# First projections in another order of x's tiles, and two sets of loads moved back

## The chip, the core and the metric

The kernel runs on one core of a Trainium2 chip. The metric is the device time of one execution in microseconds (us), given as the median of several runs. A core has five engines that each take their own instructions in order: TensorE (PE, matrix products; its weight loads are listed as PEld), VectorE (DVE), ScalarE (ACT), GpSimd (POOL) and SyncE (SP). SP here does nothing but issue DMA transfers, one after the other. The engines meet only through semaphores.

## The reference

The input x has 2048 tokens of 640 channels. Two branches are computed from it and mixed by a gate:

```python
g = _sigmoid((x * gate_w).sum(-1, keepdims=True))
a = _A_ref(x, A_wq, A_wk, A_wv, A_wo, A_beta)   # attention in 4 segments of 512 tokens, with a memory
b = _B_ref(x, B_w_r, B_w_i)                     # 2-D real FFT, times W = w_r + i*w_i, inverse FFT
return g * a + (1 - g) * b
```

Branch A has 32 heads of 20 channels. Within a segment it is causal softmax attention; beside it a linear memory of the segments before is read with phi(q) = q + 1 or exp(q), and updated with phi(k) and v. `sigmoid(beta)` weighs the two parts for each head, and a last product with `wo` closes the branch. Branch B transforms tokens and channels, multiplies by 2048 x 321 complex weights (the spectral weights), and transforms back.

## The kernel before

**How the work is cut.** Segment by segment (`s` = 0 to 3), `project` (L966) makes q, k and v from the transposed tokens `xT`, which the DMA delivers in five channel tiles `c` = 0 to 4 of 128 channels; `attend` (L1221) takes heads in groups of four: `qk_unit` (L1283) makes logits on PE, ACT takes their exponential into `ex` (L1319), POOL cuts out the causal mask (L1340), and PE multiplies by v. Branch B is spread between: `fold` (L946) adds and subtracts halves of the rows of x (`xsb`, through `xf`) on DVE and POOL, the products named `F1` (first transform, `fcat` against `xsb`) follow, then `D` and `T` (channel transform with table `big`, token transform with table `tt`), the multiplication with the spectral weights in `Wt` (L1496), and back through `Tb` and `Db`. `Db` (L1534) reads the columns of `big` from 1288 on, the inverse tables; `D` (L1480) reads the columns below.

**The first stage.** PE first runs ten products on zeros (`warm_up`, L847). Then `proj_direct` (L1017) makes q and k of the first two head groups (q0, k0, q1, k1) for segment 0, straight into the padded tile `qkp`: 4 x 5 operations named `projd`, one for each result and channel tile, the five of a result summing into one PSUM bank. Each result is copied out by one operation `ev_projd`. The weights `wq` and `wk` come in two parts: the first 192 columns (`ld_wqa`, `ld_wka`), which are all that `proj_direct` needs, and the other 448 (`ld_wqb`, `ld_wkb`), which every later projection (`proj_tile`, L1083) needs too. The x tiles come by three transposing DMAs: tiles 1 and 2 first, then tile 0, then 3 and 4, with `ld_wka` between the first two.

**beta.** `consts` (L929) takes exp(-beta) on ACT (L933) and from it, on DVE, 1 + exp(-beta) (L935), its reciprocal (L937) and their product (L938), which every copy of v (L1171) multiplies with.

**What sets the order.** All operations are recorded first and numbered in the order of recording. The table `ORDER` (from L633) is a list of numbers written out by hand: number v stands for operation v // 2, and v % 2 picks one of its engines where it may run on two (`copy_alts`: 0 is ACT, 1 is DVE). `Sched.schedule` (L117) walks it, keeps for each engine the order that the table gives, and picks PSUM banks, DMA semaphores and extra waits from its own table of costs; `emit` (L290) writes the instructions with their semaphore waits. So an engine never takes a later operation while an earlier one waits. The costs in `QUEUE` are the planner's alone; what it writes into the program for DMA is that a transfer waits for those issued some 1.6 MB ahead of it, and for the last user of its semaphore.

The programs of the engines are themselves fetched by DMA while they run, in 34 pieces of 16 KB (the queue called "instruction" in the profile); the longest by far is that of PE, with 4391 products and as many weight loads.

Of the kernel before, what the change touches and what calls it, by code (L numbers as in the profile page):

```python
# [12 lines left out]
P = 128  # L13
# [6 lines left out]
KD = 321  # L20
# [457 lines left out]
def dap(ap, off, *dims):  # L478
    return bass.AP(tensor=ap.tensor, offset=ap.offset + off, ap=[list(q) for q in dims])
# [25 lines left out]
class Kern:  # L505
# [84 lines left out]
    def dma(self, dst, src, nbytes, r, w, prio, tr=False, name="", after=(), queue="sp"):  # L590
# [24 lines left out]
        ("ld_big", 824320): (500.0, 2350.0, 16, 1350.0), ("ld_tt", 262144): (400.0, 1300.0, 16, 250.0), ("ld_tt", 524288): (400.0, 1750.0, 16, 600.0),  # L615
# [401 lines left out]
    def proj_direct(self, which, g, prio, xT, xb):  # L1017

        self.Sc.group += 1
        b = self.b  # L1020
        w, p0_ = (self.wq, 0) if which == "q" else (self.wk, 4 * L)
# [642 lines left out]
```

## Time and profile before

| what | value |
| --- | --- |
| median of 3 runs | 240.53 us |
| lowest and highest run | 238.36 and 241.71 us |
| profiled execution | span 238.5 us from first to last instruction; no other time is listed for it |
| PE busy | 94% of the span |
| ACT, DVE, POOL busy | 83%, 82%, 68% |
| mean granted clock of PE | 0.993 of full speed |
| moved by DMA | 42.18 MB in 59121 packets |

The span and the runs stand close: the profiled execution lies near the lowest of the three runs. A row of the timeline gives start, length, engine, line, the tile written and the tiles read, the shape and the number of instructions joined in the row; in brackets stands how long the engine was idle just before and what ended that. The lines L561, L571 and L573 are those of helpers (product, copy on ACT, copy on DVE), so such rows are told apart by their tiles. Successive rows of PE overlap, since products are pipelined; the distance from start to start is what one of them costs in a stream.

### The profile page before, as it was taken

Reading aid. Unit: us, or ns where it says so; the run is one execution under the profiler, and the core shown is the slowest. Engines: PE = TensorE matmul, PEld = TensorE weight load, DVE = VectorE, ACT = ScalarE, POOL = GpSimd, SP = SyncE. Lnnn points to the kernel's source line nnn. Section 1 sums busy time; section 2 is a strip of 40 time slices with the busy share of each in tenths; the row PEclk is TensorE's granted clock in tenths of the full one; section 3 lists DMA queues with packets and bytes.
Section 4 is the critical chain, followed back from the end, with each engine's and each line's share of the span. In section 5 each row is a group of like instructions: output and inputs, shape, how many; then the busy total and the mean of one; then the engine's idle time right before and its main releaser. Section 6 shows DMA issues by size and latency. Waiting matters only on the chain.

```text
span 238.5 us, 10359 instructions
## 1 busy us (share of the span) xinstructions
PE 224.9 (94%) x4391; PEld 142.1 (60%) x4391; DVE 194.8 (82%) x486; ACT 197.1 (83%) x233; POOL 162.0 (68%) x300
## 2 busy tenths in 40 slices
PE   6899999979999999999989999899999999989994
PEld 2576566656546666555657665456554456657794
DVE  0189998859999998899998888999999996847453
ACT  2079888969999998999989999988999888788820
POOL 8133139436769976737888979777998677786840
PEclk9799999999999999999999999999999999999999
DMA  7999659997879586493886683544998767492224
GB/s 148 294 330 271 196 148 171 231 230 157 230 181 231 156 214 184 122 269 100 179 230 186 182 278 87 174 124 138 200 273 210 187 142 109 95 82 85 74 70 110
DMA packets 59121, 42.18 MB, mean 177 GB/s; under 512 B 30212, under 2 KB 55364, under 8 KB 59076
## 3 DMA queue, kind: packets, MB, share of 16 engines
q1 hardware_dynamic: 58036, 40.96, 71.8%
q8 instruction: 34, 0.56, 1.0%
q10 hardware_dynamic: 1040, 0.57, 0.9%
q14 instruction: 11, 0.09, 0.1%
HBM read 23.32 MB, written 12.30 MB: 149 GB/s over the span
## 4 chain that ended last, share of the span: by engine, by line
PE 62%; ACT 13%; DMA 11%; DVE 9%; issue 2%; POOL 1%; SPq 1%; DVEq 0%; POOLq 0%
PE psum L561 54%; ACT ex L1319 11%; PE psum L559 8%; DMA qkp<-qk_scr 3%; DVE Pt L1496 2%; DMA u_scr<-ub 2%; DMA pkn<-phk 2%; DMA xT<-in_A_x_dram 2%; DMA tt<-tab_tt 2%; POOL ex L1340 1%; DMA dnc<-u_scr 1%; DVE qu L573 1%; SPq L594 1%; DVE Bt L573 1%; DVE phk L1141 1%
## 5 line engine op out<-in xcount | busy, mean ns | idle before, releaser
L1319 ACT ACTIVATE ex<-psum 128x2048 bf16<-128x2048 f32 (+4 forms) x92 | 138.5, 1506 | 13.2 <-PE psum L561 10.9
L1340 POOL TENSOR_SCALAR_AFFINE_SELECT ex<-ex 128x256 bf16<-128x256 bf16 (+2 forms) x224 | 118.6, 551 | 29.5 <-ACT ex L1319 6.1
L561 PE MATMUL psum<-qkp 20*64 20x64 bf16 (+5 forms) x1280 | 32.3, 270 | 3.5 <-ACT ex L1319 2.8
L561 PE MATMUL psum<-xT,wq 128*128 128x512 bf16 (+1 forms) x135 | 31.7, 423 | 2.3 <-DMA xT<-in_A_x_dram 2.0
L561 PE MATMUL psum<-xT,wk 128*128 128x256 bf16 (+1 forms) x280 | 32.6, 282 | 1.3 <-issue 1.3
L561 PEld LDWEIGHTS psum<-qkp 20*64 20x64 bf16 x1280 | 13.3, 103 | 21.9 <-ACT ex L1319 16.3
L1496 DVE TENSOR_TENSOR Pt<-psum,Wt 128x642 bf16<-128x642 f32 x32 | 25.4, 818 | 1.1 <-PE psum L561 0.9
L561 PE MATMUL psum<-wv,xT 128*32 128x321 bf16 (+3 forms) x390 | 26.1, 301 | 0.0
L561 PEld LDWEIGHTS psum<-xT,wk 128*128 128x128 bf16 (+1 forms) x280 | 20.5, 101 | 7.8 <-issue 4.0
L961 POOL TENSOR_TENSOR xsb<-xf 128x320 bf16<-128x320 bf16 (+2 forms) x11 | 8.1, 744 | 20.5 <-DVE xf L956 11.3
L559 PE MATMUL psum<-wo,oU 128*32 128x320 bf16 x480 | 21.5, 300 | 0.0
L573 DVE CAST ot<-psum 128x320 bf16<-128x320 f32 x22 | 10.4, 488 | 10.3 <-PE psum L559 7.2
L1171 DVE TENSOR_TENSOR va<-psum,ebx 128x320 bf16<-128x320 f32 x32 | 15.2, 487 | 4.2 <-PE psum L561 2.7
L561 PE MATMUL psum<-big,Cp 128*128 128x321 bf16 (+1 forms) x96 | 18.0, 302 | 0.2
L561 PEld LDWEIGHTS psum<-wv,xT 128*32 128x32 bf16 (+1 forms) x390 | 14.1, 96 | 6.3 <-issue 0.9
L561 PE MATMUL psum<-ex,va 128*32 128x64 bf16 (+3 forms) x576 | 17.6, 257 | 0.2
L561 PE MATMUL psum<-big,Ac 128*128 128x161 bf16 (+2 forms) x96 | 17.8, 256 | 0.0
L573 DVE CAST Bt<-psum 128x322 bf16<-128x322 f32 x28 | 14.3, 520 | 2.5 <-PE psum L561 2.3
L561 PEld LDWEIGHTS psum<-ex,va 128*32 128x32 bf16 x576 | 10.9, 96 | 8.7 <-POOL ex L1340 1.8
L561 PE MATMUL psum<-tt,Yt 128*128 128x256 bf16 (+1 forms) x96 | 15.8, 275 | 0.3 <-DVE Yt L1501 0.3
L1542 DVE TENSOR_TENSOR G<-eo,psum 128x320 bf16<-128x320 f32 x32 | 14.9, 477 | 1.2 <-ACT eo L571 0.5
L561 PEld LDWEIGHTS psum<-xT,wq 128*128 128x128 bf16 (+1 forms) x135 | 9.8, 105 | 10.2 <-DMA xT<-in_A_x_dram 2.5
(98 smaller groups left out, 392.0 us busy)
## 6 DMA issues: line engine op xcount, KB each, us to landing
qkp<-qk_scr SPq DMA_DIRECT2D x28, 160.0 KB
tt<-tab_tt SPq DMA_DIRECT2D x8, 512.0 KB, 4.5
qk_scr<-qu SPq DMA_DIRECT2D x12, 256.0 KB, 2.8
u_scr<-ub SPq DMA_DIRECT2D x12, 256.0 KB, 3.1
xsb<-in_A_x_dram SPq DMA_DIRECT2D x8, 320.0 KB, 5.0
oU<-u_scr SPq DMA_DIRECT2D x15, 128.0 KB, 3.6
out_dram<-ot SPq DMA_DIRECT2D x12, 160.0 KB
Wt<-in_B_w_r_dram SPq DMA_DIRECT2D x16, 80.2 KB, 4.7
```

Of the source, the lines that this page charges most:

```text
L559: h = e.matmul(dst, wt, r_, start=st, stop=sp_, **{**kw, "tile_position": (0, q), "skip_group_check": True})
L561: h = e.matmul(o_, l_, r_, start=st, stop=sp_, **kw)
L573: alts["dve"] = (lambda e: e.tensor_copy(dst(), src()), 67 + 1.04 * n, 68.0)
L594: return e.dma_start_transpose(d_, s_)
L961: self.either(lambda e, dst=dst, src=src, d0=d0, n=n, op=op: e.tensor_tensor(xs.ap(o + dst, [D, 2], [1, n]), xf.ap(src + d0, [321, 2], [1, ...
L1141: fmin = lambda e: e.tensor_tensor(dst(), dst(), et.ap(0, [1, L]), ALU.min)
L1171: self.one("dve", lambda e: e.tensor_tensor(va.ap(i * H * VW + h0 * VW, [VW, nh], [1, DH]), self.ps(bank, 0, [DH, nh], [1, DH]), self.ebx. ...
L1319: self.one("act", lambda e, d=d, q=q: e.activation(self.ex.ap(*d), self.ps(bank, *q), ACT.Exp, scale=SC), n, [bank], [self.exb(s, 2 * pr + ...
L1340: self.one("pool", lambda e: e.affine_select(self.ex.ap(e0 + d0, [1280, 4], [1, n], np_=np_), self.ex.ap(e0 + s0, [1280, 4], [1, n], np_=np_),
L1496: self.one("dve", lambda e, ri=ri, Pt=Pt, Wt=Wt, wo_=wo_, bank=bank: e.tensor_tensor(Pt.ap(ri * 322, [644, 2], [1, KD]), self.ps(bank, 0, ...
L1542: self.one("dve", lambda e, q=q, n2=n2, bank=bank, eo=eo: e.tensor_tensor(self.G.ap(n2 * D + 639 * q, [1 - 2 * q, 320]), eo.ap(q, [1, 320] ...
```

## The change

In `proj_direct` the five channel tiles are summed in the order 1, 2, 0, 3, 4; the start and stop flags of the sum follow the position and not the tile:

```diff
-        for c in range(5):
+        for step, c in enumerate((1, 2, 0, 3, 4)):
...
-                                c == 0 and o == 0, c == 4, {"tile_position": (0, 32 * hh), "skip_group_check": True})
+                                step == 0 and o == 0, step == 4, {"tile_position": (0, 32 * hh), "skip_group_check": True})
...
-            self.mms(items, [b("w" + which + "a"), xb[c], bank], [], prio + (0.0 if c < 3 else 0.45), name="projd", mode=2)
+            self.mms(items, [b("w" + which + "a"), xb[c], bank], [], prio + (0.0 if step < 3 else 0.45), name="projd", mode=2)
```

The load of `big` becomes two, and `Db` now waits for the second:

```diff
-        self.dma(lambda: self.big.ap(0, [1, 3220]), lambda: dap(self.tab["big"].ap(), 0, [3220, P], [1, 3220]),
-                 P * 6440, [], [self.b("big")], 5.0, name="ld_big")
+        self.dma(lambda: self.big.ap(0, [1, 1288]), lambda: dap(self.tab["big"].ap(), 0, [3220, P], [1, 1288]),
+                 P * 2576, [], [self.b("big")], 5.0, name="ld_big")
...
+        self.dma(lambda: self.big.ap(1288, [1, 1932]), lambda: dap(self.tab["big"].ap(), 1288, [3220, P], [1, 1932]),
+                 P * 3864, [], [self.b("inv")], 50.0, name="ld_inv")
...
-                    self.mms([(th, KD)], cpb + [b("big"), bank], [], prio, name="Db", mode=0)
+                    self.mms([(th, KD)], cpb + [b("inv"), bank], [], prio, name="Db", mode=0)
```

`ORDER` is written anew. The new load shifts the numbers of all later operations, so nearly every line of the table differs; operation by operation, the order of each engine changes only in this:

- **PE**: before, the twenty `projd` stand as q0 t0, k1 t0, q1 t0, k0 t0, q1 t1, q0 t1, k0 t1, q1 t2, q0 t2, q0 t3, k1 t1, k0 t2, k0 t3, k0 t4, q0 t4, k1 t2, k1 t3, k1 t4, q1 t3, q1 t4 (t is the channel tile). After: tiles 1 and 2 of q0, q1, k0, k1 in turn, then tile 0 of q0, k0, q1, k1, then tiles 3 and 4 of q0, k0, q1, k1. All that follows is the same.
- **ACT**: the copy of q1 moves here from DVE, between the copy of k0 and the first exponential. The exp(-beta) at L933, which stood right behind the first exponential, now stands behind the second; the copy of a k tile and an exp for phi (L1128) lie between.
- **DVE**: the copy of q0 stands ahead of the first two operations of `fold` instead of behind them; the copy of q1 is gone; all else is the same.
- **POOL**: no change.
- **SP**: three of the spectral loads `ld_W` for the second pair of row groups move back: two from right behind `ld_big` to behind the second tile pair of the third segment's xT, and one from behind `ld_hm` to behind the first store of `ub` (L1255). The new `ld_inv` stands some twenty transfers further, between the last pad load of the second segment's first half and the next `ld_W`.

More of the change, by code (lines that the diff above doesn't have):

```diff
@@ L614 @@
         ("ld_W", 41088): (600.0, 250.0, 16, 450.0), ("ld_W", 82176): (600.0, 500.0, 16, 550.0), ("ld_big", 659456): (500.0, 1750.0, 16, 950.0),
-        ("ld_big", 824320): (500.0, 2350.0, 16, 1350.0), ("ld_tt", 262144): (400.0, 1300.0, 16, 250.0), ("ld_tt", 524288): (400.0, 1750.0, 16, 600.0),
+        ("ld_big", 329728): (500.0, 950.0, 16, 1000.0), "ld_inv": (500.0, 1400.0, 16, 1000.0), ("ld_tt", 262144): (400.0, 1300.0, 16, 250.0), ("ld_tt", 524288): (400.0, 1750.0, 16, 600.0),
         ("ld_u", 131072): (595.0, 650.0, 16, 450.0), ("ld_u", 655360): (595.0, 1700.0, 16, 1800.0), ("ld_u", 262144): (595.0, 1000.0, 16, 900.0),
@@ L1027, in proj_direct, with th @@
                 for o, n, src in self.token_order(which, xT, c):
-                    def th(c=c, hh=hh, o=o, n=n, src=src):
+                    def th(c=c, hh=hh, o=o, n=n, src=src, step=step):
                         return (self.ps(bank, o, [1, n], p0=32 * hh, np_=32), w.ap(c * D + (4 * g + hh) * DH, [1, 32]), src(),
-                                c == 0 and o == 0, c == 4, {"tile_position": (0, 32 * hh), "skip_group_check": True})
+                                step == 0 and o == 0, step == 4, {"tile_position": (0, 32 * hh), "skip_group_check": True})
                     items.append((th, n / 4))
             items.sort(key=lambda q: q[0].__defaults__[2])
-            self.mms(items, [b("w" + which + "a"), xb[c], bank], [], prio + (0.0 if c < 3 else 0.45), name="projd", mode=2)
+            self.mms(items, [b("w" + which + "a"), xb[c], bank], [], prio + (0.0 if step < 3 else 0.45), name="projd", mode=2)
         self.Sc.op(self.copy_alts(lambda: pad.ap(p0_ + g * L, [1, L]), lambda: self.ps(bank, 0, [1, L]), L),
```

196 rows, old and new, of the table ORDER are left out of this document.

## The prediction

> **What bounds the kernel now.** I read the page first, then the chain that ended last in order of time, then the timeline engine by engine over the two stretches that the change touches.
>
> ```profile
> span 238.5 us, 10359 instructions
> PE 224.9 (94%) x4391; PEld 142.1 (60%) x4391; DVE 194.8 (82%) x486; ACT 197.1 (83%) x233; POOL 162.0 (68%) x300
> PEclk9799999999999999999999999999999999999999
> PE 62%; ACT 13%; DMA 11%; DVE 9%; issue 2%; POOL 1%; SPq 1%; DVEq 0%; POOLq 0%
> ```
>
> PE is busy for 94% and holds 62% of the chain. The clock digit falls only in the second slice (6 to 12 us). With every engine's order fixed, a delay taken out early is worth its length at the end, unless another engine's queue gives it back. So the question is what each part takes out, and what stands behind it.
>
> ```profile
> 2.80 4.09 DMA xT<-in_A_x_dram
> 6.94 29.51 PE psum L561 x425
> ...
> 50.80 1.30 issue
> ```
>
> Two early places stand in the chain: PE has its first x tile at 6.94, and at 50.80 it waits 1.30 us for nothing that the profile shows.
>
> **Part 1, the order of the tiles.** PE's rows, from the warm-up to the first FFT products:
>
> ```profile
> 1.30 3.67 PE L561 MATMUL psum<-G 128*128 128x512 bf16 x10 [1.30 <-DVE G L852]
> 6.94 0.40 PE L561 MATMUL psum<-xT,wq 128*32 128x512 bf16 x4 [1.97 <-DMA xT<-in_A_x_dram]
> ...
> 8.16 1.08 PE L561 MATMUL psum<-xT,wq 128*32 128x512 bf16 x8
> ...
> 11.88 0.83 PE L561 MATMUL psum<-xT,wk 128*32 128x256 bf16 x24
> 12.54 0.61 PE L561 MATMUL psum<-xT,wq 128*32 128x512 bf16 x8
> 13.08 0.43 PE L561 MATMUL psum<-qkp 20*64 20x512 bf16 x12
> 13.44 3.23 PE L561 MATMUL psum<-xT,wk 128*128 128x256 bf16 x28
> 16.60 0.42 PE L561 MATMUL psum<-qkp 20*64 20x320 bf16 x16
> 16.95 2.36 PE L561 MATMUL psum<-xT,wk 128*128 128x256 bf16 x20
> 19.15 0.39 PE L561 MATMUL psum<-fcat,xsb 128*128 128x128 bf16 x4
> ```
>
> ```profile
> 7.00:8.00 1.00, 1.00 (x24) 0.61 (x28) 0.00 (x0) 0.00 (x0) 0.00 (x0) 0.73 0.96 233
> 8.00:9.00 1.00, 1.00 (x16) 0.46 (x12) 0.00 (x0) 0.00 (x0) 0.00 (x0) 0.50 0.94 269
> ...
> 11.00:12.00 1.00, 1.00 (x42) 0.88 (x37) 0.00 (x0) 0.11 (x1) 0.92 (x2) 1.00 1.02 370
> ```
>
> The second fence is busy time in stretches of 1 us; the third number from the end is the clock. After the idle 1.97 us before 6.94 it is halved for some 3.4 us. One `projd` takes 0.22 us from start to start at full clock (three of k between 11.88 and 12.54), about 0.43 at half.
>
> The tiles 1 and 2 are issued first, so they can be summed before tile 0 lands. No row gives their landing; it lies between the end of the warm-up (1.30 + 3.67 = 4.97) and 6.94, and I take 5.0, since SP issued them 2 us before tile 0. Then PE goes on without its gap, the clock stays full, and twenty `projd` (4.4 us) with a short wait for `ld_wka` end near 9.7. The first logits follow at 9.7 instead of 13.08, 3.4 us earlier.
>
> That gain is cut twice. **First cut:** the 28 products behind them need `ld_wkb`.
>
> ```profile
> DMA packets 51, 0.11 MB, mean 368 GB/s; under 512 B 4, under 2 KB 10, under 8 KB 51
> ...
> DMA packets 77, 0.16 MB, mean 398 GB/s; under 512 B 15, under 2 KB 15, under 8 KB 77
> ```
>
> These are the packets of 11.0 to 11.3 and of 11.3 to 11.7. `ld_wkb` moves rows of 448 columns, 896 B; six packets between 512 B and 2 KB are left in the first stretch, none in the second. So it lands after 11.3 and before 13.44; I take 11.7, near its last packets. The 28 products start there: the 3.4 us become 13.44 - 11.75 = 1.7, and PE idles some 1.6 us before them. The second logits move from 16.60 to 14.9.
>
> **Second cut:** beta. ACT's rows, then DVE's:
>
> ```profile
> 11.89 0.60 ACT L571 ACTIVATE qkp<-psum 128x512 bf16<-128x512 f32 x1 [9.37 <-PE psum L561]
> 13.60 1.88 ACT L1319 ACTIVATE ex<-psum 128x2048 bf16<-128x2048 f32 x1 [1.11 <-PE psum L561]
> 15.38 0.22 ACT L933 ACTIVATE ebx<-beta 128x32 f32<-128x32 bf16 x1
> ...
> 16.68 0.63 ACT L1128 ACTIVATE et<-q 128x512 bf16<-128x512 bf16 x1
> 17.21 1.86 ACT L1319 ACTIVATE ex<-psum 128x2048 bf16<-128x2048 f32 x1
> ```
>
> ```profile
> 9.67 1.03 DVE L956 TENSOR_TENSOR xf<-xsb 128x640 bf16<-128x640 bf16 x2 [8.43 <-DMA xsb<-in_A_x_dram]
> ...
> 16.70 0.69 DVE L573 CAST q<-psum 128x512 bf16<-128x512 f32 x1 [0.84 <-PE psum L561]
> 17.31 0.17 DVE L935 TENSOR_SCALAR ebx<-ebx 128x32 f32<-128x32 f32 x1
> ...
> 18.64 0.32 DVE L961 TENSOR_TENSOR xsb<-xf 128x318 bf16<-128x318 bf16 x1
> ```
>
> Before, exp(-beta) was done at 15.60, long before DVE came to L935 at 17.31. Now it stands behind the second exponential. That follows the second logits (14.9 + 0.42) and the phi exp: in the old rows it starts 0.61 us after them (17.21 - 16.60), so now at 15.5; it ends at 17.4, and exp(-beta) at 17.6. DVE comes to L935 at 15.7 and waits there until 17.6, 0.25 us **later** than before. Queued behind it are phi's max, the folds up to that at 18.64 and the copies of the first FFT. DVE has no gap from 16.70 to 19.57, so all of this slides by 0.25 us. PE, which would reach its product of fcat and xsb at 17.5, waits for that fold: 18.64 + 0.32 + 0.25 = 19.2, against 19.15. So at 19.2 PE stands where it stood, after a second idle stretch of 1.6 us, and the start is worth between 0.1 and 0.25 us of loss. I take **+0.2**; below, the loss is bounded by the rivals.
>
> The copies cost nothing: q0's on DVE (0.69, as at 16.70) fits ahead of the x rows that release 9.67, q1's on ACT (0.60, as at 11.89) ends before the first logits do.
>
> **Part 2, the loads.** Around the wait at 50.80:
>
> ```profile
> 52.10 0.39 PE L561 MATMUL psum<-xT,wk 128*128 128x256 bf16 x2 [1.30 <-issue]
> ```
>
> ```profile
> q1 hardware_dynamic: 690, 1.17, 107.9%
> ...
> q8 instruction: 1, 0.02, 5.6%
> ...
> big<-tab_big SPq DMA_DIRECT2D x1, 805.0 KB, 7.8
> ```
>
> The first two lines are DMA queues from 45.0 to 49.3 (no instruction packet among them) and from 49.3 to 50.8; the last is from the list of DMA issues. From 45.0 to 49.3 the engines moved 1.17 MB of kernel data at full share, then the 16 KB of instructions, and PE went on at 52.10. I read the wait as an instruction fetch that stood behind the queued loads, `ld_big` above all. Its new size is 1288/3220 of 805 KB, 322 KB: 483 KB less, and at 1.17 MB in 4.3 us (272 GB/s) that is 1.8 us earlier for what stands behind. That covers the 1.30.
>
> ```profile
> 42.42 0.52 SPq L596 DMA_DIRECT2D Wt<-in_B_w_r_dram  x1
> 42.98 1.33 SPq L596 DMA_DIRECT2D Wt<-in_B_w_i_dram  x2
> ...
> 46.97 0.59 SPq L596 DMA_DIRECT2D tt<-tab_tt  x1
> ...
> 74.97 0.54 SPq L596 DMA_DIRECT2D qkp<-qk_scr  x1
> 77.37 0.47 SPq L596 DMA_DIRECT2D Wt<-in_B_w_i_dram  x1
> ```
>
> Against it: two spectral loads fewer behind `ld_big` bring SP some 1.3 us ahead (42.42 to 43.7), and with it `tt` (512 KB). If the fetch is asked for after `tt` is issued at 45.7, it waits for 512 KB instead of 483 and nothing is gained. The value lies between 0 and **-1.3**; I take -1.3. The three moved loads fill `Wt` for a row group whose multiplication comes some 20 us later, and their issues (0.5 to 0.7 us each) fall where SP waits for copies, so they cost nothing; without that cover, 0.6 us each. `ld_inv` stands between the transfers at 74.97 and 77.37: SP is free for 1.86 us there, against an issue of 0.5 to 1.35 (the old `ld_big`). Its 483 KB are needed by `Db` past 160 us. If they push an instruction fetch near 78 back, that costs up to the same 1.8 us less its slack.
>
> **Sum:** 238.5 + 0.2 - 1.3 = 237.4 for the profiled execution. The median lies 2.0 above that span, so 240.53 - 1.1 = **239.4 us**.
>
> **Rivals.**
>
> 1. *The start gain survives*: exp(-beta) doesn't hold DVE, because the second logits come sooner or DVE finds slack before 28 us. Against it: DVE's gapless rows. It adds the 1.7 us: 237.5.
> 2. *The wait at 50.80 stays*, because the fetch never stood behind `ld_big`, or stands behind `tt` now: 240.7. The Trainium skill, "DMA: Bandwidth & Descriptors", section "Queues, rings and completion order", says that each DMA engine takes turns between the queues it has work for, packet by packet; by it a smaller `ld_big` wouldn't move the fetch at all. The trace leans the other way: no instruction packet in 4.3 us of full queues.
> 3. *Slower: the clock halves after the new gaps.* Part 1 turns one gap of 1.97 us into two of 1.6 (before 11.7 and before 19.2). The old gap was followed by 3.4 us at half clock, the gap of 1.30 at 50.80 by none (its slices read 9). If 1.6 us is enough, each drop costs half of 3.4, 1.7 us; the first delays the second logits, and with them exp(-beta) and all of DVE. One drop: 241.1. Two: 242.8. The Trainium skill, "TensorE: Matmul & The Clock Gate", section "Part 1: The HAM clock gate", puts the fall at an idle window of about 3.4 us; by it this rival is dead. The trace doesn't agree: 1.97 us sufficed.
> 4. *The planner's by-product*: it picks banks and semaphores anew for the whole program. No row prices that; the chain's DMA and issue shares, 13% or 31 us, are where it would show. It may fall on either side of 2% (4.8 us).
>
> **Chances.** Forecast 0.38; rival 1 0.13; rival 2 0.16; rival 3 0.14; rival 4 0.19, of it 0.11 faster than 235.7 and 0.08 slower than 245.3. The first four lie between 237.5 and 242.8 and hold 0.81; with the spread of the runs before (1.2 up, 2.2 down) around the ends the range is 235.6 to 243.6. About 2% is what a measurement of this kernel tells from no change. From the cases: faster 0.12, same 0.78, slower 0.10 (one per cent each way for rivals 1 and 3 with the run spread on top).
>
> **What would show it.** PE's first product on xT near 5.0, no second slice at 7; PE idle some 1.6 us before the 28 products at 11.7; DVE idle 1.9 us ahead of L935, released by ACT at 17.6; fcat times xsb near 19.2 as before; no "issue" wait near 50 us, and the stretches from 52 on 1.1 us earlier. I am wrong if L935 doesn't wait, if the clock falls again after 11.7, or if the wait at 50.80 comes back behind `tt`.

## The result, and the profile after

The changed kernel takes 240.14 us (median of 19 runs, 238.39 to 241.46) against 239.12 us (19 runs, 236.94 to 241.71) for the kernel before on the same chip: a ratio of 1.0052, with a 95% interval of 1.0029 to 1.0074. It is slower by 1.0 us by the medians and 1.2 us by the ratio, where 1.1 us faster was forecast. The profiled execution took 241.13 us, its span is 239.4 us. Lines behind L912 have moved down by two: exp(-beta) is L935, DVE's first step on it L937, `fold` L958 and L963, the exponential L1321.

The page's row for PE's clock, as for the kernel before:

```profile
PEclk9997999999999999999999999999999999999999
```

The clock's dip has moved from the second slice to the fourth. PE's rows of the timeline show the start (idle time and its releaser in brackets):

```profile
4.93 1.05 PE L561 MATMUL psum<-xT,wq 128*32 128x512 bf16 x16
...
10.23 0.43 PE L561 MATMUL psum<-qkp 20*64 20x512 bf16 x12
12.43 3.23 PE L561 MATMUL psum<-xT,wk 128*128 128x256 bf16 x28 [1.77 <-DMA wk<-in_A_wk_dram]
15.59 0.42 PE L561 MATMUL psum<-qkp 20*64 20x320 bf16 x16
...
19.93 0.40 PE L561 MATMUL psum<-fcat,xsb 128*128 128x128 bf16 x4 [1.62 <-DVE xsb L963]
...
21.65 2.73 PE L561 MATMUL psum<-wv,xT 128*128 128x320 bf16 x24
24.31 0.52 PE L561 MATMUL psum<-qkp 20*64 20x320 bf16 x16
```

PE begins on x at 4.93 instead of 6.94 and has the first logits out at 10.23 instead of 13.08. Then it waits 1.77 us for `ld_wkb`, and 1.62 us for the fold. What holds the fold is seen on ACT and DVE:

```profile
16.21 1.86 ACT L1321 ACTIVATE ex<-psum 128x2048 bf16<-128x2048 f32 x1
17.96 0.22 ACT L935 ACTIVATE ebx<-beta 128x32 f32<-128x32 bf16 x1
```

```profile
18.21 0.18 DVE L937 TENSOR_SCALAR ebx<-ebx 128x32 f32<-128x32 f32 x1 [1.82 <-ACT ebx L935]
...
19.55 0.32 DVE L963 TENSOR_TENSOR xsb<-xf 128x318 bf16<-128x318 bf16 x1
```

So PE stands at 19.93 where it stood at 19.15: 0.78 us late. Behind it, the record of before has these rows:

```profile
20.63 1.50 PE L561 MATMUL psum<-wv,xT 128*128 128x320 bf16 x24
22.07 0.42 PE L561 MATMUL psum<-qkp 20*64 20x320 bf16 x16
```

The same products of wv and x that took 1.50 us there take 2.73 in the changed kernel, since its clock is halved (stretches of 3.42 us of the changed kernel; the third number from the end is the clock):

```profile
17.74:21.16 3.42, 1.80 (x30) 1.17 (x27) 2.94 (x10) 1.80 (x5) 0.57 (x1) 1.00 1.14 276
21.16:24.58 3.42, 3.42 (x39) 1.65 (x44) 2.51 (x8) 2.50 (x3) 1.61 (x3) 0.50 1.14 342
```

The unit that starts at 22.07 before starts at 24.31 now: the delay has grown to 2.24 us. Of it 0.9 us come back at the wait that part 2 aimed at, which is 0.36 us long instead of 1.30:

```profile
42.03 6.13 DMA qkp<-qk_scr
48.16 0.04 issue
48.21 4.84 PE psum L561 x113
53.05 0.36 issue
53.41 6.70 PE psum L561 x75
```

These are rows of the chain that ended last (start, length, what). PE goes on at 53.41 instead of 52.10, and the span ends 0.9 us later.

### The profile page after: what moved, and what is told of

The parts are those of the page before. It is cut to its first block, busy times and chain, and to the rows that moved or that the text cites. A ratio compares the mean times of both kernels' runs of the same rounds, so it can differ in the third digit from the quotient of the medians.

```text
span 239.4 us, 10362 instructions
## 1 busy us (share of the span) xinstructions
PE 225.4 (94%) x4391; PEld 141.6 (59%) x4391; DVE 194.9 (81%) x485; ACT 197.7 (83%) x234; POOL 162.2 (68%) x300
## 4 chain that ended last, share of the span: by engine, by line
PE 62%; ACT 16%; DMA 9%; DVE 7%; SPq 2%; issue 1%; POOL 1%; DVEq 0%; POOLq 0%
PE psum L561 56%; ACT ex L1321 13%; PE psum L559 6%; DMA wk<-in_A_wk_dram 3%; DMA qkp<-qk_scr 3%; DMA pkn<-phk 2%; SPq L594 2%; DMA out_dram<-ot 2%; POOL ex L1342 1%; DVE Pt L1498 1%; ACT eo L571 1%; DVE qu L573 1%; DVE ot L573 1%; SPq L596 0%; DVE G L1544 0%
## 5 line engine op out<-in xcount | busy, mean ns | idle before, releaser
L1321 ACT ACTIVATE ex<-psum 128x2048 bf16<-128x2048 f32 (+4 forms) x92 | 138.5, 1505 | 15.3 <-PE psum L561 13.2
L561 PE MATMUL psum<-xT,wk 128*128 128x256 bf16 (+1 forms) x280 | 32.0, 273 | 2.4 <-DMA wk<-in_A_wk_dram 2.0
L561 PE MATMUL psum<-xT,wq 128*128 128x512 bf16 (+1 forms) x135 | 30.2, 381 | 0.6 <-DVE Cp L573 0.3
L561 PE MATMUL psum<-wv,xT 128*32 128x321 bf16 (+3 forms) x390 | 27.5, 311 | 0.0
L561 PEld LDWEIGHTS psum<-xT,wk 128*128 128x128 bf16 (+1 forms) x280 | 20.0, 97 | 8.6 <-DMA wk<-in_A_wk_dram 2.7
L963 POOL TENSOR_TENSOR xsb<-xf 128x320 bf16<-128x320 bf16 (+2 forms) x11 | 8.3, 758 | 24.1 <-DVE xf L958 13.2
L561 PE MATMUL psum<-ex,va 128*32 128x64 bf16 (+3 forms) x576 | 17.6, 257 | 0.3
L1130 ACT ACTIVATE et<-qu 128x512 bf16<-128x512 bf16 x25 | 15.3, 624 | 0.1
```

The costliest lines, as they stand in the source:

```text
L561: h = e.matmul(o_, l_, r_, start=st, stop=sp_, **kw)
L963: self.either(lambda e, dst=dst, src=src, d0=d0, n=n, op=op: e.tensor_tensor(xs.ap(o + dst, [D, 2], [1, n]), xf.ap(src + d0, [321, 2], [1, ...
L1130: self.one("act", lambda e: e.activation(et.ap(0, [1, L]), qsl(), ACT.Exp), L, [qb], [b("et", pi_)], late, fix=95, name="phi_exp")
L1321: self.one("act", lambda e, d=d, q=q: e.activation(self.ex.ap(*d), self.ps(bank, *q), ACT.Exp, scale=SC), n, [bank], [self.exb(s, 2 * pr + ...
```

## The experiments

All ratios are to the kernel before, timed on the same chip in the same session, with 95% intervals. e1 to e4 ran on one chip, e5 to e7 on a second, e8 to e11 and e12 to e14 in two sessions on a third; between these groups only ratios can be compared.

| kernel | ratio | interval |
| --- | --- | --- |
| e1: changed kernel, exp(-beta) back behind the first exponential | 1.0004 | 0.9967 to 1.0042 |
| e2: before, part 1 alone (tiles, with the late exp(-beta)) | 1.0074 | 1.0036 to 1.0112 |
| e3: before, part 2 alone (loads) | 0.9996 | 0.9953 to 1.0038 |
| e4: changed kernel, eight idle products in PE's second gap | 1.0150 | 1.0102 to 1.0198 |
| e5: before, exp(-beta) alone behind the second exponential | 1.0009 | 0.9974 to 1.0045 |
| e6: before, PE doesn't wait for the first pads | 0.9964 | 0.9931 to 0.9996 |
| e7: e1, PE doesn't wait for the first pads | 0.9881 | 0.9840 to 0.9921 |
| e8: e1, pads first in SP's row | 0.9892 | 0.9857 to 0.9928 |
| e9: before, pads first | 1.0007 | 0.9976 to 1.0037 |
| e10: changed kernel, pads first | 0.9964 | 0.9931 to 0.9996 |
| e11: e8 with the loads of before | 0.9981 | 0.9954 to 1.0009 |
| e12: e9 with POOL's waits as in before | 0.9937 | 0.9904 to 0.9970 |
| e13: e11 with POOL's waits as in before | 0.9919 | 0.9887 to 0.9952 |
| e14: e8, exp(-beta) between phi's exp and the second exponential | 0.9882 | 0.9837 to 0.9928 |

### The two parts and the place of exp(-beta)

e1 puts one number of `ORDER` back; the rest of the changed kernel stays:

```diff
 ACT's order (540 and 580 are the first two exponentials, 268 the k copy, 270 phi's exp, 66 exp(-beta))
-540, 268, 270, 580, 66
+540, 66, 268, 270, 580
```

> The changed kernel with one operation put back: exp(-beta) stands again right behind the first exponential on ACT. Theory 1 (exp(-beta) behind the second exponential holds DVE, the folds behind it hold PE, and the new gap of PE halves the clock): L937 doesn't wait on DVE, the first product of fcat and xsb starts at 18.5 to 19.0 instead of 19.93, no half clock between 20 and 25, and the time is 1.0 to 2.5 us under that of the changed kernel, some 0.990 to 0.997 of the kernel before. Theory 2 (the moved loads cost the time): as the changed kernel, 1.005. Theory 3 (banks and semaphores, picked anew): anything, with no tie to the wait at L937.

e2 and e3 make the two parts alone. In e2 the order of the sum, and with it PE's, ACT's and DVE's order, is that of the changed kernel, and the loads are those of before; in e3 it is the other way round:

```diff
-        for step, c in enumerate((1, 2, 0, 3, 4)):
+        for step, c in enumerate(range(5)):
```

> The kernel before with the first part alone: the order of the tiles, the copies, and exp(-beta) behind the second exponential; the loads as they were. Theory 1: slower than the changed kernel by the wait near 50 us that comes back, so 1.007 to 1.012 of the kernel before; DVE waits some 1.8 us ahead of L935 and PE some 1.6 us for the fold. Theory 2: no slower than before, 0.995 to 1.001.

> The changed kernel with the first part undone: tiles in the order 0 to 4 and PE, ACT and DVE in the order of the kernel before; the loads moved. Theory 1: the wait of PE near 50 us is 0 to 0.4 us instead of 1.30, 0.994 to 0.998 of the kernel before. Theory 2: 1.003 to 1.008. If the fetch of instructions never stood behind the load of big, the wait is there and the ratio is 1.000.

e4 gives PE work in the gap before the product of fcat and xsb, to see whether the clock then stays full:

```diff
+        bank = Bank(1, "gen")
+        self.mms([(lambda: (self.ps(bank, 0, [1, L]), self.wk.ap(0, [1, P]), self.xT[0].ap(0, [1, L]), True, True, {}), L)] * 8,
+                 [bank], [], 0.0, name="fill")
```

> The changed kernel with eight products of 128x512 into a bank that nobody reads, put on PE ahead of the first product of fcat and xsb, where PE is idle for 1.6 us; the waits stay. If the half clock after that gap costs time (theory 1): DVE still waits 1.8 us at L937 and the product still starts at 19.9 to 20.1, but the clock is full from 20 to 25, and the time is 0.4 to 1.4 us under the changed kernel, 0.999 to 1.003 of before. If the clock is no part of it: the same as the changed kernel or up to 0.2 us more, 1.005.

Measured: e2 as expected, 1.0074. e1 is a miss: it lies under the changed kernel (1.0004 against 1.0052, in intervals that overlap), but only comes level with the kernel before. e3 shows no gain either, though its wait near 50 us is gone. e4 is a miss and settles nothing: its clock stayed full and the product came at 19.62, but its record then has waits of 1.35 us from 38.31 (for a pad), 1.02 from 51.34 and 2.18 from 79.54. Why it is slower than the changed kernel stays open.

In e1 DVE doesn't wait, PE has the product 1.98 us sooner than in the record of before, and then loses it. Its rows on DVE and PE, and those of its chain:

```profile
15.31 0.33 DVE L937 TENSOR_SCALAR ebx<-ebx 128x32 f32<-128x32 f32 x1
```

```profile
17.17 0.40 PE L561 MATMUL psum<-fcat,xsb 128*128 128x128 bf16 x4
...
37.33 0.42 PE L561 MATMUL psum<-qkp 20*64 20x320 bf16 x16 [1.41 <-DMA qkp<-qk_scr]
45.51 0.43 PE L561 MATMUL psum<-qkp 20*64 20x512 bf16 x12 [0.56 <-DMA qkp<-qk_scr]
50.99 0.39 PE L561 MATMUL psum<-xT,wk 128*128 128x256 bf16 x2 [0.64 <-issue]
```

```profile
6.01 5.34 DMA wk<-in_A_wk_dram
11.36 0.04 issue
11.40 14.96 PE psum L561 x156
...
30.99 0.21 DVE phq L1142
31.20 0.52 SPq L594
...
38.97 6.49 DMA qkp<-qk_scr
```

The chain leaves PE at 26.4, goes through DVE's folds and phi, and from 31.2 to 38.97 it is SP, issuing one transfer after the other, that ends last: a store, the transposing transfers of phi(k) (L594), and the pad loads. In e3's record PE waits for a pad, too:

```profile
47.36 0.43 PE L561 MATMUL psum<-qkp 20*64 20x512 bf16 x12 [1.41 <-DMA qkp<-qk_scr]
```

That pad was issued at 39.80, against 39.69 in the record of before, but took 7.51 us to land instead of 6.23, so here it isn't SP's row that is late.

e1's chain gave theory S, which the next runs test: **SP's row of issues sets when the pads land, and PE's head start ends there.**

### Is the pads' row the wall?

> The kernel before once more, for a record in which TensorE's clock isn't halved after its first gap. Theory S: between 31 and 46 us the row of SP's stores and pad loads is what PE waits for in the end, and a PE that comes early only waits longer there. Then, with the clock full from 7 us on, PE reaches the unit at 37.8 about 1 us sooner and its wait for the pads (0.27 us in the first record) grows to 0.8 to 1.4 us. Rival F: an early gain or loss goes through to the end, and the pads matter only by chance. Then that wait stays below 0.5 us and the span is 1.5 us shorter or more.

A second record of the kernel before, with the clock full from 5.87 us on:

```profile
7.46 0.40 PE L561 MATMUL psum<-xT,wq 128*32 128x512 bf16 x4 [1.72 <-DMA xT<-in_A_x_dram]
...
12.28 3.23 PE L561 MATMUL psum<-xT,wk 128*128 128x256 bf16 x28
...
17.99 0.39 PE L561 MATMUL psum<-fcat,xsb 128*128 128x128 bf16 x4
...
37.74 0.42 PE L561 MATMUL psum<-qkp 20*64 20x320 bf16 x16 [1.08 <-DMA qkp<-qk_scr]
51.47 0.39 PE L561 MATMUL psum<-xT,wk 128*128 128x256 bf16 x2 [1.25 <-issue]
```

In the first record the unit at 37.74 stands here:

```profile
38.08 0.42 PE L561 MATMUL psum<-qkp 20*64 20x320 bf16 x16 [0.27 <-DMA qkp<-qk_scr]
```

As theory S says: PE is 1.16 us earlier at the product of fcat and xsb than in the first record, and waits 1.08 us for the pads instead of 0.27. SP's rows for the last seven pad loads of that unit, of the second record and of the first:

```profile
32.56 3.85 SPq L596 DMA_DIRECT2D qkp<-qk_scr  x7
```

```profile
32.09 4.48 SPq L596 DMA_DIRECT2D qkp<-qk_scr  x7
```

SP is done with them at 36.41 and at 36.57: what PE does earlier hardly reaches it in this record. It isn't so in every record. In e7, described below, which leaves SP's row as it is, PE has the product at 18.28, 0.87 us earlier than in the first record of before, and SP's row comes forward with it:

```profile
31.28 4.45 SPq L596 DMA_DIRECT2D qkp<-qk_scr  x7
```

The seven loads end there at 35.73, 0.84 us earlier. From the product to their end it is 17.42 us in the first record and 17.45 in e7, but 18.42 in the second record and 18.69 in e1. In these last two a fetch of instructions stretches three of SP's stores by some 1.5 us, at 22.16 and at 21.73 (see the end). So in these records it is the fetch that keeps SP's row back while PE is early; no run moves the fetch alone to test it.

The records correct the base of the prediction, too. The 28 products start at 11.68 to 12.28 in the four records with the old order of the tiles in which PE ran the first projections at full speed (e5, e12, e6 and the second of before), and at 11.40 to 12.57 in the ten with the new order, there right behind the landing of `ld_wkb`. So against these four the tile order gains nothing, where the forecast had 1.7. The 13.44 of the first record belongs to a start at half speed, as do e3's 13.55 and e9's 14.01.

e5 moves exp(-beta) alone, in the kernel before:

```diff
-538, 64, 266, 268, 578
+538, 266, 268, 578, 64
```

> The kernel before with one operation moved: exp(-beta) from behind the first exponential to behind the second; tiles and loads as before. The second exponential ends at 19.07 in the record of before, so exp(-beta) at 19.2, DVE's next step on it at 19.3 instead of 17.31, and the product of fcat and xsb at 20.9 to 21.1 instead of 19.15. If that place alone is the fault: +1.2 to +1.9 us, ratio 1.005 to 1.008. If the fault is the order of the tiles or the clock: ratio 1.000.

It costs nothing (1.0009), the value expected if the place were not at fault, but not for that reason. DVE waits 1.83 us and PE has the product at 19.18, 1.2 us later than in the second record, but then it finds the pads landed: there is no wait at 37 us in e5's record. The wait for the pads hides the loss as it hides the gain. In the record of the changed kernel it doesn't: there PE comes to that product at 19.93, and the halved clock follows.

e6 and e7 take PE's wait for the pads away; in segment 0, head groups 2 to 5 read the padded tiles of groups 0 and 1:

```diff
-            pidx, gl = (2 * s + g // 4) % self.NPAD, g % 4
+            pidx, gl = ((2 * s + g // 4) % self.NPAD, g % 4) if s or g > 5 else (0, g % 2)
```

> The kernel before, but in segment 0 the products of q and k for head groups 2 to 5 read the padded tiles of groups 0 and 1, which PE has anyway, in place of those that the pad loads bring; the pad loads are still issued. So the output is wrong for these groups, and PE doesn't wait for these pads. Theory S (the pads' row takes an early start away): PE came to the pads nearly in time in the record of before (waits of 0.27 and 0.26), so little is gained: ratio 0.996 to 0.999. Rival F: 1.000.

> The changed kernel with exp(-beta) back behind the first exponential, and with the same cut as in the run without pad waits of the kernel before: in segment 0, groups 2 to 5 read the tiles of groups 0 and 1, so their output is wrong, and PE doesn't wait for these pads. Theory S: the early start of 1.98 us at the first product of fcat and xsb, which waits of 1.41 and 0.56 for the pads had eaten, now goes through: ratio 0.990 to 0.994, and 1.2 to 2.0 us faster than the kernel before without pad waits. Rival F: 1.000, as with the pads.

Both came as theory S has it: 0.9964 and 0.9881 (a little more than the 0.990 to 0.994 expected), the second 1.4 us faster than the first (medians 236.65 and 238.07) on the one chip, in intervals that don't meet. Without the wall, the order of the tiles and the loads are worth that much together; with it, e1 shows nothing. Of the 1.4, the two records have 1.0 at the wait near 50 us (1.66 in e6, 0.66 in e7) and none at the start.

### A step that moves the wall

The second and third transposing transfers of phi(k) stand between the pad loads and hold SP for 1.25 us each, while phi(k) is wanted only by the memory, much later. e8 puts them behind the pads; e9 and e10 do it in the kernel before and in the changed one; e11 is e8 with the old loads:

```diff
 SP's order (328 to 322 pad2, 404 to 406 pad, 320 and 402 the transposing transfers)
-328, 320, 332, 336, 324, 330, 334, 326, 322, 1942, 404, 410, 408, 402, 406
+328, 332, 336, 324, 330, 334, 326, 322, 320, 1942, 404, 410, 408, 406, 402
```

> A candidate whose output is whole: the changed kernel with exp(-beta) back behind the first exponential, and in SP's row the second and third transposing transfers of phi(k) put behind the pad loads of segment 0 instead of between them (each holds SP for 1.25 us). Theory S, the pads' row holds PE: the wait near 36 us shrinks by up to 1.25 and the one near 45 us goes; 1.2 to 2.4 us faster than the kernel before, ratio 0.990 to 0.995. If the pads wait for the stores of q and k to land and not for SP's row: 1.000, as without it.

> The kernel before with the same step in SP's row alone: the second and third transposing transfers of phi(k) behind the pad loads. By theory S it takes away what the full-clock record of before waits near 37 us (1.08), and nothing where PE is late anyway: ratio 0.996 to 0.999, 0.8 to 1.5 us slower than the candidate, since the tiles' order and the loads can come through there only.

> The changed kernel with the same step in SP's row, exp(-beta) left behind the second exponential. Its PE is late at the pads (first product of fcat and xsb at 19.93 against 17.17 with exp(-beta) in front), so the step brings little: ratio 1.001 to 1.005. Against the candidate it is 1.5 to 2.5 us slower, the price of the one moved operation once nothing hides it.

> The candidate with the loads of the kernel before: one load of the whole table big, the three spectral loads where they were. If the smaller first load takes the wait near 50 us away and nothing gives it back, this is 0.6 to 1.3 us slower than the candidate, ratio 0.994 to 0.998. If the loads are worth nothing here either, it is equal to the candidate within 0.4 us.

e8 is 1.1% faster than the kernel before (2.5 us by the medians, a little over the range) and has no wait for a pad; PE's only wait over 0.2 us between 30 and 57 us is this:

```profile
41.60 1.54 PE L561 MATMUL psum<-wv,xT 128*128 128x321 bf16 x10 [0.49 <-DVE qu L573]
```

e10 is a miss on the good side: even with exp(-beta) late the step brings the changed kernel from 1.0052 to 0.9964. Against e8 the late exp(-beta) costs 0.7%, 1.4 us by the medians (237.43 and 236.01), a little under the 1.5 to 2.5 expected; and here the two intervals don't meet. e11 is 2.0 us slower than e8 (238.05 against 236.01), more than the 0.6 to 1.3 expected. e9 missed: nothing gained. Its record names what stands in the way, POOL's step on the gate and, behind it, PE:

```profile
57.81 0.22 POOL L1044 TENSOR_SCALAR gate<-gate 128x4 f32<-128x4 f32 x1 [2.33 <-DVE phk L1140]
```

```profile
62.66 0.73 PE L561 MATMUL psum<-ex,va 128*32 128x512 bf16 x24 [1.07 <-POOL ex L1340]
```

In the kernel before POOL does this step without a wait. The program of e9 says so: beside the data's own waits, `schedule` makes POOL wait for whatever DVE operation (of those marked `lock`) its costs place just ahead, and for six POOL operations that choice came out differently in e9 and e11 than in the kernel before. e12 and e13 set the six back:

```diff
+                keep = {307: 1002, 311: 1003, 314: 501, 313: None, 400: None, 1118: None}
+                if o.id in keep:
+                    o.dyn += [ops[keep[o.id]]] if keep[o.id] else []
-                if ldv is not None:
+                elif ldv is not None:
                     o.dyn.append(ldv)
```

> The kernel before with the pads first in SP's row, and POOL's six waits on DVE that the planner had drawn anew for that row set back to those of the kernel before (in the record with the new ones, POOL stands 2.33 us ahead of its step on the gate at 57.81, and PE 1.07 us ahead of its product at 62.7). If that by-product ate the step's gain: 1.0 us faster than without, ratio 0.995 to 0.998, and no wait of PE near 62. If the pads' row is worth nothing for the kernel before: 1.000.

> The candidate with the loads of the kernel before, and POOL's six waits as in the kernel before. If the 2.0 us that the old loads cost the candidate are the planner's waits on POOL (1.07 us seen at 60.20): ratio 0.990 to 0.994, level with the candidate. If it is the loads: 0.997 to 0.999, no better than with the new waits.

Both gained, as expected for the by-product: 0.9937 (better than its range) and 0.9919. The same step in e12's record:

```profile
53.54 0.22 POOL L1047 TENSOR_SCALAR gate<-gate 128x4 f32<-128x4 f32 x1
```

So six waits that nobody asked for cost 1.45 us (238.70 against 237.25) in the one pair and 1.5 us (238.05 against 236.53) in the other; the two sessions have the kernel before at 238.56 and 238.47, and in neither pair do the intervals meet. With them out of the way, the start is worth 0.7 us (e12 237.25, e13 236.53) and the loads 0.5 us (e13, e8 236.01), both in intervals that overlap: neither is shown to be more than nothing. The wait near 50 us is 0.69 us in e13's record and absent in e8's.

e14 places exp(-beta) once more, behind phi's exp and ahead of the second exponential, since its input lands only at 14.2 to 15.1:

```diff
-540, 66, 268, 270, 580
+540, 268, 270, 66, 580
```

> The candidate with exp(-beta) one place later on ScalarE: behind the phi exp and ahead of the second exponential. Its input lands between 14.2 and 15.1, so right behind the first exponential ACT waits 1.2 us for it; behind the phi exp (some 15.5) it waits for nothing, DVE has it by 15.7 and the product of fcat and xsb stays near 17.2. 0 to 0.5 us faster than the candidate, ratio 0.987 to 0.991; if DVE is held by it after all, slower by up to 1 us.

```profile
15.58 0.63 ACT L1130 ACTIVATE et<-q 128x512 bf16<-128x512 bf16 x1
16.11 0.21 ACT L935 ACTIVATE ebx<-beta 128x32 f32<-128x32 bf16 x1
16.23 1.86 ACT L1321 ACTIVATE ex<-psum 128x2048 bf16<-128x2048 f32 x1
```

ACT neither waits for beta nor holds DVE up by the length of an exponential. The ratio is 0.9882 (median 235.91 of 6 runs), level with e8 and 1.2% under the kernel before.

## Why the prediction was wrong

**Part 1, start:** right in kind. First product near 5.0 (4.93), the first cut by `ld_wkb` and the idle time ahead of the 28 products (1.6 forecast, 1.77 measured). I read the landing as 11.7; it was 12.38 (6.03 + 6.35 in its chain), and 11.36 in e1. So 0.7 us of the 1.7 weren't there, and against the second record, at full clock, none of it was (12.43 and 12.28). The base was at fault: I took 3.4 us of halved clock in one record as part of the kernel.

**Part 1, second cut:** right in kind, too small. DVE waited for ACT at L937 as foretold (1.82 us; forecast 1.9), but came out at 18.21 instead of 17.6, because everything ahead hung on the later `ld_wkb`. The term **+0.2** measured +0.78. e2 has part 1 without the loads (1.0074). That the place of exp(-beta) costs time is shown by e8 and e10; e1's 0.5% under the changed kernel lies in intervals that overlap.

**Rival 3, the clock:** one drop happened, at the second gap and not at the first. The price of 1.7 us measured 2.24 - 0.78 = 1.46. It isn't in every run: of the 19 runs of the changed kernel nine have a mean clock of 0.993, like the record, and average 240.5 us; the other ten average 239.7. So it explains some 0.4 us (nine nineteenths of 0.8) of the 0.7 between the means of the 19 runs (240.06 and 239.40), or less, since the kernel before has such runs too: 17 of the 103 that were timed beside the experiments have a mean clock of 0.993 or lower. One drop was a possibility to which all of rival 3 gave 0.14; it came in about half of the runs.

**Part 2:** the wait at 50.80 fell by 0.94 where 1.30 was forecast, and in time it brought nothing by itself (e3, 0.9996). In e3's record a pad that landed 7.51 us after its issue, instead of 6.23, held PE for 1.41 us. Whether the moved loads delayed it or chance did isn't settled by one record. Nor is it shown that the size of `ld_big` set the wait: with the old loads it is 0.69 us in e13, 0.36 in e9 and absent in e11, and with the new ones 0.64 in e1 and 1.02 in e4. That it is a wait for a fetch fits the records: a packet of instructions starts at 49.39 and PE goes on at 52.10 before, at 50.33 and 53.41 in the changed kernel.

**The step that failed** is the sum, 238.5 + 0.2 - 1.3. The +0.2 became +0.78 at the product of fcat and xsb and, where the clock fell, 1.46 more, which the sum had at nothing. The -1.3 became 0.94 at its wait in the record, and nothing in the time where the loads were moved alone (e3). Behind both terms stands the sentence "a delay taken out early is worth its length at the end, unless another engine's queue gives it back". I looked for that queue on DVE and stopped at 19 us. It was SP's, at 31 to 39 us, and its row stood in the chain that I had read: `DMA qkp<-qk_scr` from 39.69 on. Without PE's wait for these loads the start and the loads gain 1.4 us (e7 against e6), with it nothing (e1). A wait of only 0.26 us behind it looked harmless, since in that record PE came late, its clock having been halved. Rival 1 ("the start gain survives") had the same hole: e1 met its condition and brought nothing, for this reason.

**Rival 4, the planner's by-product:** not seen in the change itself, where only two of POOL's waits on DVE differ, but real: 1.5 us in e9 and e11, near the size of everything else here. PSUM banks and DMA semaphores are drawn anew in the changed kernel as well; no run separates what that costs.

**The range:** its ends don't follow from its figures, since 237.5 - 2.2 and 242.8 + 1.2 are 235.3 and 244.0 and not 235.6 and 243.6. The measured 240.14 lies inside either.

## What to carry to other kernels

Follow an early gain to the next place where PE meets the row of another engine, and ask there whether that row comes forward as well; the length of today's wait doesn't tell. Here it came forward in some records (e7) and was held back in others (e1), and a wait of 0.3 us became one of 1.4. Read the start of a kernel from two records before pricing it, since a clock that fell in one of them makes a gain appear that other runs don't have to give. And where a planner writes the waits, compare them operation by operation after each reordering: an edit can be right and be paid for elsewhere.

## What the runs showed of the hardware

**The clock falls after some short gaps and not after others.** Idle stretches of 2.10 us (e9), 1.97 us (the first record of before) and 1.62 (the changed kernel, e2) were followed by 3.41 to 3.42 us at half clock. Each lay whole in one of the stretches of 3.41 us that the clock's changes mark. But the 1.74 us in e12 (5.14 to 6.88) lay whole in one too, from 4.39 to 7.80, and the clock stayed full. Of the 1.72 us in the second record of before 1.59 lay in one such stretch, and it stayed full as well:

```profile
5.87:9.28 3.41, 1.82 (x48) 1.26 (x52) 0.00 (x0) 0.00 (x0) 0.00 (x0) 1.00 1.18 239
9.28:12.69 3.41, 3.41 (x96) 2.39 (x89) 2.73 (x5) 0.84 (x2) 2.10 (x3) 1.00 1.02 324
```

In the changed kernel's stretch before the fall PE was busy for 1.80 us, here for 1.82 and in e12's for 1.67, so neither the gap nor the busy time alone draws the line; what does stays open. Two gaps lay across the border of two stretches, and the clock stayed full: the 1.62 us of e5 (17.56 to 19.18, with a border at 18.15, counted on from 4.50), and even 2.22 us in e7 (10.35 to 12.57, with a border at 11.45, counted on from 4.62). Where the stretches begin differs from run to run: the first change of the clock in a record lies anywhere from 4.04 to 10.47 us. The Trainium skill, "TensorE: Matmul & The Clock Gate", section "Part 1: The HAM clock gate", says that the window runs freely and that its phase varies between runs, and the traces agree; it puts the fall at an idle window of about 3.4 us, and the 1.62 us here speak against that.

**An instruction fetch that falls on SP's stores stretches them.** Three stores of q take SP 1.64 us at 21.78 in the first record of before, and in e1:

```profile
21.73 3.11 SPq L596 DMA_DIRECT2D qk_scr<-q  x3
```

```profile
q8 instruction: 1, 0.02, 13.8%
```

The second fence is from the list of DMA queues between 21.3 and 21.8 us of e1: a packet of instructions started there, at 21.43. Between 21.3 and 23.2 us of before there is none, and in the second record of before one starts at 21.96 and the three stores take 3.10 us. The 17 records agree. In six of them (these two, e6, e8, e12, e13) the packet starts between 0.30 us before the first of the three stores and 1.16 us behind it, and they take 2.55 to 3.13 us. In the eleven others it starts 1.29 us behind it or later, and they take 1.64 to 1.67 us. So a fetch that falls on SP's stores costs its row up to 1.5 us. Six of the seven records in which PE has the product of fcat and xsb before 18.0 us are among the hit ones, and none of the ten others is. So in these records an early PE mostly goes with a fetch on these stores, and with it the pads that PE waits for are kept back.
